# Five staging tiles instead of three for the first ten projection blocks of a transformer block

## The chip, the cores and the metric

The kernel runs on one core of a Trainium2 chip. The metric is the device time of one launch in microseconds (us): 2104.36, the median of three runs (2101.28 to 2106.47). The engines are called by their profile names where rows are read: PE is TensorE's matmul, PEld its weight load, DVE VectorE, ACT ScalarE, POOL GpSimd, SP SyncE. ACT and SP issue the DMAs of this kernel; SPq and ACTq in a row mean the issuing of a DMA by that engine.

## The reference

One pre-LayerNorm transformer block on a sequence of 2048 tokens of width 640: attention with 32 heads of width 20, then a SwiGLU feed-forward part of width 1728.

```python
def _A_ref(x, wqkv, wo):
    qkv = (x @ wqkv).reshape(B, S, 3, H, Dh).transpose(2, 0, 3, 1, 4)
    q, k, v = qkv[0], qkv[1], qkv[2]
    scores = jnp.einsum("bhqd,bhkd->bhqk", q, k) * (Dh ** -0.5)
    o = jnp.einsum("bhqk,bhkd->bhqd", _softmax(scores), v)
    return o.transpose(0, 2, 1, 3).reshape(B, S, D) @ wo
def _B_ref(x, w_gate, w_up, w_down):
    return (_silu(x @ w_gate) * (x @ w_up)) @ w_down
h = x + _A_ref(_layernorm(x), A_wqkv, A_wo)
return h + _B_ref(_layernorm(h), B_w_gate, B_w_up, B_w_down)
```

## The kernel before

Values in float32 are split into a high and a low part (`split`, L84: ACT copies the high part, another engine subtracts it for the low part), and a product is made of three matmuls: high by high, low by high, high by low.

The change lies in the first stage, the projections (L268 to L617). The 2048 tokens go through in four chunks (`c`, 0 to 3) of `CH` = 512. For each chunk the tokens are normalised on DVE (`norm`, L387), turned so that the width lies on the partitions (`flip`, L407; `flip_tokens`, L416, for the first chunk) and kept as two tiles `z_hi` and `z_lo` (`zs[c]`). From these come ten blocks of 128 rows of keys and queries (`query_key`, L434, 15 matmuls of 128x512; the first two blocks are made in `first_blocks`, L454), and eight half-tiles of values (`value`, L508, 15 matmuls of 128x320). A chunk has 18 slots, one for each piece of that work (`slot[0]`, L573); in chunk 0 slot 1 has no work, because blocks 0 and 1 are made in slot 0. Blocks have even numbers for keys and odd ones for queries.

*Staging tiles.* A finished block lies in a PSUM bank. `keep` (L469) takes the next staging tile from the list `es` (`next_e`, L264, pops the first and puts it at the end), copies the bank into it with ACT, splits it there into high and low, and queues its stores to the scratch tensors `q_d` and `k_d` in DRAM. Key blocks of chunks 0 and 1 also keep the difference of their two halves (`over`). Before slot 8 ACT and DVE split straight from PSUM; from slot 8 on ACT makes one copy first (L487) and POOL makes the low part. `flip` takes a staging tile too, as the place of its plain copy (L414, L281), and ACT and POOL read it right away; no DMA does. `es` has three tiles: `e0`, `e1` and a view on `v_stk0`, called `third`. In the fourth chunk `third` leaves the list and a tile of the pool's `z_hi` comes in (L570, L571).

```python
        def next_e():
            es.append(es.pop(0))
            return es[-1]
```

*Order of the stores.* `store` (L428) issues the pieces queued by the call before. So the stores of block m are issued when block m + 1 is kept. Up to slot 9 they go to SP's queue, later to ACT's (L505).

*Early maxima.* Scattered among these matmuls stand those of the score maxima. `visit` (L363) is called after each slot, and within a value or a block of later chunks; each call does up to two or three pairs. A pair is two matmuls into a double bank `ps_wide` (three of them). Pairs of the first head group use the full width, and DVE reduces 2x512 scores (`max_pair`, L171, L180); the others use the kept half sums and differences (`max_halves`, L182): ACT copies a half through relu (L193), DVE adds and reduces (L195). Their keys and queries are loaded back from `k_d` and `q_d` by SP into four `raw` tiles and the tile `fifth` (`load_items`, L302; `stack`, L141; L148). Four tiles of `raw` also hold the raw weights in the first slots (`load_w`, L373).

*What orders the work.* The program order on each engine is that of the calls; each engine takes its instructions strictly in that order, SP and ACT their DMA instructions as well. A tile is written again only after the reads of its former content, a store among them, have ended. [...]

After the projections come the attention with its output projection (PE and ACT), and the feed-forward part (PE), with PE nearly always busy.

Of the kernel before, what the change touches and what calls it, by code (L numbers as in the profile page):

```python
# [11 lines left out]
F32R = mybir.dt.float32r  # L12
# [5 lines left out]
P = 128  # L18
# [5 lines left out]
ND = D // P  # L24
NT = S // P
CH = 512
NC = S // CH
# [17 lines left out]
def tile_block(ctx: ExitStack, tc: tile.TileContext, x, wqkv, wo, wg, wu, wd, out):  # L45
# [30 lines left out]
    def ps_one():  # L76
        return psum.tile([P, CH], F32, name="ps_one", tag="ps_one", bufs=2)
# [6 lines left out]
    def split(src, hi, lo, lo_engine=nc.vector):  # L84
        nc.scalar.activation(hi, src, AF.Copy)  # L85
        lo_engine.tensor_tensor(out=lo, in0=src, in1=hi.bitcast(F32), op=ALU.subtract)  # L86

    def rstd_steps(pool, var, n, tag):

        v = pool.tile([P, n], F32, name="v_" + tag)  # L90
        r = pool.tile([P, n], F32, name="r_" + tag)
        t = pool.tile([P, n], F32, name="t_" + tag)

        def some(f, *args, **kw):
            return lambda: f(*args, **kw)

        ts, tt = nc.vector.tensor_scalar, nc.vector.tensor_tensor
        guess = [
            some(ts, v, var, EPS, None, op0=ALU.add),
            some(  # L100
                ts, r.bitcast(I32), v.bitcast(I32), -0.5, 1597463007.0, op0=ALU.mult, op1=ALU.add
            ),
        ]
        better = [
            some(tt, out=t, in0=r, in1=r, op=ALU.mult),
            some(tt, out=t, in0=t, in1=v, op=ALU.mult),
            some(ts, t, t, -0.5, 1.5, op0=ALU.mult, op1=ALU.add),
            some(tt, out=r, in0=r, in1=t, op=ALU.mult),
        ]
        return r, guess + better * 3  # L110
# [7 lines left out]
    def stats(pool, src, mv):  # L118
        st = pool.tile([P, 2, 6], F32, name="st")
        for i in range(2):  # L120
            nc.vector.bn_stats(st[:, i, :], src[:, i * HALF : (i + 1) * HALF])
        nc.vector.bn_aggr(mv, st)
# [29 lines left out]
    def load_keys(g, cs):  # L152

        k = keys[g] = k_stk[g % 2]
        stack(k[:, :, cs], 1, g, cs.start // CH)
# [103 lines left out]
    EW = CH + CH // 2  # L259
    es = [evp.tile([P, 2, EW], F32R, name=f"e{i}", bufs=1) for i in range(2)]  # L260
    es.append(v_stk[0].rearrange("p t w -> p (t w)")[:, : 2 * EW].bitcast(F32R))
    third = es[2] = es[2].rearrange("p (i n) -> p i n", i=2)

    def next_e():  # L264
        es.append(es.pop(0))
        return es[-1]

    with tc.tile_pool(name="pa", bufs=2) as pa:  # L268
        xs = {}
        zs = {}  # L270
# [3 lines left out]
        def load_x(c):  # L274
            for t in range(c * TPC, (c + 1) * TPC):
                xs[t] = pa.tile([P, D], F32, name="xt", tag="xt", bufs=4)
                nc.sync.dma_start(xs[t], x[t * P : (t + 1) * P, :])

        def split_sbuf(src, hi, lo, copy):

            nc.scalar.activation(copy, src, AF.Copy)  # L281
            split(copy, hi, lo, nc.gpsimd)
# [90 lines left out]
        def load_w(i):  # L373

            m, n = 2 * i, min(2, 3 * ND - 2 * i)
            raw = raw_tile().bitcast(F32)
            for j in range(n):
                raws[m + j] = raw[:, :, j * P : (j + 1) * P]
            nc.sync.dma_start(
                raw[:, :, : n * P], wqkv[:, m * P : (m + n) * P].rearrange("(k p) n -> p k n", p=P)  # L380
            )

        def split_w(m):
            cs = slice(m * P, (m + 1) * P)
            split(raws.pop(m), w_hi[:, :, cs], w_lo[:, :, cs])

        def norm(c):  # L387

            mv = pa.tile([P, TPC, 2], F32, name="mv")
            r, steps = rstd_steps(pa, mv[:, :, 1], TPC, "a")  # L390

            def apply(t):
                nc.vector.tensor_scalar(
                    xs[c * TPC + t], xs[c * TPC + t], mv[:, t, 0:1], r[:, t : t + 1],
                    op0=ALU.subtract, op1=ALU.mult,
                )

            zs[c] = (
                pa.tile([P, ND, CH], F32R, name="z_hi"), pa.tile([P, ND, CH], F32R, name="z_lo")
            )  # L400
            return (
                [lambda t=t: stats(pa, xs[c * TPC + t], mv[:, t, :]) for t in range(TPC)]
                + [lambda f=f, g=g: (f(), g()) for f, g in zip(steps[::2], steps[1::2])]
                + [lambda t=t: apply(t) for t in range(TPC)]
            )

        def flip(c, k):  # L407
            ps = ps_one()
            for t in range(TPC):
                nc.tensor.transpose(  # L410
                    ps[:, t * P : (t + 1) * P], xs[c * TPC + t][:, k * P : (k + 1) * P], ident
                )
            z_hi, z_lo = (z[:, k, :] for z in zs[c])
            split_sbuf(ps, z_hi, z_lo, next_e()[:, 0, :CH].bitcast(F32))  # L414
# [35 lines left out]
        def finish_keep():  # L450
            while halved:
                halved.pop(0)()

        def first_blocks(*hns):  # L454

            if not firsts:
                firsts.extend(ps_one() for _ in range(2))
            z_hi, z_lo = zs[0]
            for h, n in hns:
                cols = slice(h * CH // 2, (h + 1) * CH // 2)  # L460
                a, w = ((z_hi, w_hi), (z_lo, w_hi), (z_hi, w_lo))[n]
                for m, ps in enumerate(firsts):
                    for k in range(ND):
                        nc.tensor.matmul(
                            ps[:, cols], w[:, k, m * P : (m + 1) * P], a[:, k, cols],
                            start=(h == n == k == 0), stop=(h == 1 and n == 2 and k == ND - 1),
                        )
# [71 lines left out]
            nc.tensor.matmul(warm, ident, xs[TPC - 1][:, :CH], start=True, stop=True)  # L539
        for f in norm(0):  # L540
            f()
        first_raw = raws.pop(0), raws.pop(1)
        for m, raw in enumerate(first_raw):
            nc.scalar.activation(w_hi[:, :, m * P : (m + 1) * P], raw, AF.Copy)
# [19 lines left out]
        for c in range(NC):  # L564
            lns = []
            work = (some_keys + some_queries if c else first) + parts
            if c == NC - 1:
                work = some_keys + parts + some_queries

                es[:] = [e for e in es if e is not third]  # L570
                es.insert(1, pa.tile([P, ND, CH], F32R, name="z_hi")[:, :2])  # L571
            for j, (kind, *which) in enumerate(work):
                slot[0] = 18 * c + j  # L573
                if c == 0 and j < 9:
                    for i in range(split_at[j], split_at[j + 1]):
                        split_w(i + 2)
                        if i % 2 == 1 and loaded < 8:
                            load_w(loaded)
                            loaded += 1
                if j == 0 and c + 1 < NC:  # L580
                    if c > 0:
                        load_x(c + 1)
                    lns = norm(c + 1)
                if which:
                    if (c, j) == (0, 0):
                        first_blocks((0, 1), (1, 0), (1, 1), (0, 2), (1, 2))
                        for m, ps in enumerate(firsts):
                            keep(0, m, ps)
                    else:
                        (query_key if kind == "block" else value)(c, *which)  # L590
                visit(2 if kind == "value" or slot[0] < 10 else 3)
                finish_keep()
                if c == 0 and j == 6:
                    for ev in evs:
                        nc.gpsimd.memset(ev, 1.0)
                if j == (4 if c == 0 else 3):
                    load_keys(0, slice(c * CH, (c + 1) * CH))
                if j == (4 if c == 0 else 8) and c < 3:
                    load_queries(c)
                if 0 in ends:  # L600
                    finish_at = min(finish_at, slot[0] + 2)
                    if slot[0] == finish_at:
                        max_finish(0)
                if j == 14 and c == 3:
                    load_values(0)
                for _ in range(2 if j >= 5 else 1):
                    if j >= 1 and lns:
                        lns.pop(0)()
                if c + 1 < NC and 0 <= j - flip_at[c] < ND:
                    flip(c + 1, j - flip_at[c])  # L610
                if c == NC - 1 and j == 11:
                    nc.scalar.activation(
                        pa.tile([P, 1], F32, name="exp_table"), eps_t, AF.Exp
                    )
# [425 lines left out]
    for u in range(NU):  # L1040
        g, c = divmod(u, NC)
# [3 lines left out]
        for kt in range(NT):  # L1045
# [51 lines left out]
            k = 2 * (u - NU + 8)  # L1097
# [574 lines left out]
```

## Time and profile before

| | |
|---|---|
| runs | 2106.47, 2101.28, 2104.36 us; median 2104.36 |
| span of the profiled execution (first to last instruction) | 2102.6 us; its own time is not listed beside the span |
| mean granted PE clock | 0.996 of full speed |
| first chunk, slots 0 to 17 | ends near 97.8 us, where the first block of chunk 1 starts (PE L440 at 97.78) |
| projections | end near 388 us, where PE's attention rows (L964) begin |
| DMA | 305.38 MB in all, a mean of 145 GB/s |

A row of the timeline gives the start in us, the busy time, engine, line, operation, the tiles written and read, their shapes, the number of merged instructions, and in brackets how long the engine stood before and what released it. A row of the waits says which engine waited for which: total us, how often, and the longest.

### The profile page before, as it was taken

To read this page: it belongs to the slowest core of one execution; us is meant where nothing else is said; L and a number is where in the kernel's file an instruction comes from. 1 tells how busy PE (TensorE), PEld (TensorE's weight loads), DVE (VectorE), ACT (ScalarE), POOL (GpSimd) and SP (SyncE) were. 2 spreads that over 40 slices of the span, in tenths; PEclk is the share of its full clock that TensorE was granted. 3 is DMA by queue.
4 is the path that set the end of the run, shared out by engine and by line. 5 is a ranking of instruction groups with operands and counts; after the bars stand their busy time and mean duration, and the time that the engine had idled before them with its cause. 6 is when DMAs were issued, how large, how long until landed. Compare 5 with 4: busy or idle time off the path is not lost.

```text
span 2102.6 us, 37159 instructions
## 1 busy us (share of the span) xinstructions
PE 2063.2 (98%) x12636; PEld 1204.5 (57%) x12636; DVE 1659.2 (79%) x3631; ACT 1444.6 (69%) x2835; POOL 691.8 (33%) x949
## 2 busy tenths in 40 slices
PE   8899999999999999999999999999999999999998
PEld 6656566443333343333333333335578888888888
DVE  7677867788888888888888988887358666666677
ACT  4556575899999999999999999996743222212221
POOL 2131210234443434353420001001145444753555
PEclk9999999999999999999999999999999999999999
DMA  8575544335263443443631213132137755884542
GB/s 256 165 230 168 175 127 132 85 115 154 88 184 101 148 138 124 148 147 122 187 124 57 52 32 94 34 94 83 35 122 274 257 176 183 300 302 157 196 153 92
DMA packets 197285, 305.38 MB, mean 145 GB/s; under 512 B 47440, under 2 KB 82256, under 8 KB 196072
## 3 DMA queue, kind: packets, MB, share of 16 engines
q1 hardware_dynamic: 186168, 280.18, 42.0%
q10 hardware_dynamic: 10928, 22.82, 3.5%
q8 instruction: 102, 1.67, 0.3%
q14 instruction: 87, 0.71, 0.1%
HBM read 203.82 MB, written 98.30 MB: 144 GB/s over the span
## 4 chain that ended last, share of the span: by engine, by line
PE 88%; DVE 4%; DMA 3%; issue 1%; ACT 1%; POOL 1%; SPq 1%; ACTq 0%; POOLq 0%; DVEq 0%
PE acc L974 24%; PE ps_one L964 16%; PE ps_a L1135 15%; PE ps_max L204 12%; PE ps_b L1229 8%; PE ps_one L516 3%; PE ps_one L440 3%; PE ps_wide L188 3%; DVE over L195 2%; PE ps_max L695 2%; PE ps_b L695 1%; PE ps_wide L440 1%; DMA k_d<-e 1%; DMA halves<-j_d 1%; DVE mx L180 1%
## 5 line engine op out<-in xcount | busy, mean ns | idle before, releaser
L970 ACT ACTIVATE probs<-ps_one 128x512 f32<-128x512 f32 x2048 | 1056.7, 614 | 62.5 <-PE ps_one L964 37.1
L210 DVE TENSOR_REDUCE mx<-ps_max 128x1 f32<-128x512 f32 x1472 | 925.9, 684 | 108.2 <-PE ps_one L964 75.6
L964 PE MATMUL ps_one<-q_stk,k_stk 62*128 62x512 f32 x2048 | 586.1, 450 | 2.5 <-DVE m L86 1.8
L974 PE MATMUL acc<-probs,v_stk 128*32 128x512 f32 x4096 | 545.2, 604 | 0.0
L964 PEld LDWEIGHTS ps_one<-q_stk,k_stk 62*128 62x128 f32 x2048 | 251.3, 184 | 431.5 <-ACT probs L970 397.2
L204 PE MATMUL ps_max<-k_stk,q_stk 60*128 60x512 f32 x1472 | 380.8, 425 | 0.0
L204 PEld LDWEIGHTS ps_max<-k_stk,q_stk 60*128 60x128 f32 x1472 | 271.6, 186 | 25.3 <-DVE mx L210 1.2
L195 DVE CUSTOM_DVE_ANT_0 over<-ps_wide,over 128x256 f32<-128x256 f32 x512 | 185.4, 420 | 86.3 <-ACT over L193 85.9
L1350 DVE TENSOR_TENSOR tmp<-ps_a,tmp 128x512 f32<-128x512 f32 x208 | 141.1, 689 | 119.7 <-PE ps_a L1135 93.9
L193 ACT ACTIVATE over<-ps_wide 128x512 f32<-128x512 f32 x256 | 139.1, 597 | 90.5 <-PE ps_wide L188 44.1
L1229 PE MATMUL ps_b<-halves,yp 128*128 128x320 f32 x1032 | 179.3, 308 | 1.9 <-POOL yp L86 1.2
L974 PEld LDWEIGHTS acc<-probs,v_stk 128*32 128x32 f32 x4096 | 80.6, 108 | 175.4 <-issue 166.8
L1229 PEld LDWEIGHTS ps_b<-halves,yp 128*128 128x128 f32 x1032 | 165.1, 188 | 18.6 <-POOL yp L86 1.5
L1009 POOL TENSOR_TENSOR o<-o,rb 128x512 f32<-128x512 f32 x31 | 39.9, 1287 | 411.5 <-DMA q_stk<-q_d 163.6
L1135 PE MATMUL ps_a<-t,units 128*128 128x512 f32 x624 | 162.6, 396 | 0.0
L1135 PE MATMUL ps_a<-z,units 128*128 128x512 f32 x516 | 133.8, 394 | 0.0
L1135 PEld LDWEIGHTS ps_a<-t,units 128*128 128x128 f32 x624 | 112.6, 188 | 18.6
L86 POOL TENSOR_TENSOR yp<-y,yp 128x256 fp32r<-128x256 f32 x96 | 60.3, 628 | 188.0 <-ACT yp L85 188.0
L1234 DVE TENSOR_TENSOR h<-ps_b,h 128x320 f32<-128x320 f32 x248 | 110.0, 481 | 6.9 <-PE ps_b L1229 5.4
L1135 PEld LDWEIGHTS ps_a<-z,units 128*128 128x128 f32 x516 | 93.1, 187 | 15.9
L85 ACT ACTIVATE yp<-tmp 128x512 fp32r<-128x512 f32 x40 | 25.3, 632 | 103.2 <-POOL tmp L1222 103.2
L1135 PE MATMUL ps_a<-z,lasts 128*128 128x512 f32 x324 | 92.5, 393 | 0.0
(193 smaller groups left out, 2216.4 us busy)
## 6 DMA issues: line engine op xcount, KB each, us to landing
units<-w_d SPq DMA_DIRECT2D x186, 256.0 KB
w_d<-stage SPq DMA_DIRECT2D x106, 256.0 KB
halves<-j_d SPq DMA_DIRECT2D x70, 320.0 KB
j_d<-stage SPq DMA_DIRECT2D x42, 320.0 KB
k_stk<-k_d SPq DMA_DIRECT2D x64, 160.0 KB
q_stk<-q_d SPq DMA_DIRECT2D x64, 160.0 KB
rb<-r_d SPq DMA_DIRECT2D x32, 256.0 KB
raw<-k_d SPq DMA_DIRECT2D x42, 160.0 KB
```

The source lines that it names most:

```text
L193: nc.scalar.activation(over, ps[:, :, CH // 2 :], AF.Relu)
L195: nc.vector.tensor_tensor_reduce(over[:, b], ps[:, b, : CH // 2], over[:, b], 1.0, LOWEST, ALU.add, ALU.max, mx[:, b, pair, t, kc : kc + 1],)
L204: nc.tensor.matmul(ps, queries[u][rows, pair, t * P : (t + 1) * P], keys[u // NC][rows, pair, kc * CH : (kc + 1) * CH], start=True, stop=True,
L210: nc.vector.tensor_reduce(mxs[u][:, b, pair, t, kc : kc + 1], ps, axis=AX.X, op=ALU.max)
L440: nc.tensor.matmul(ps, w[:, k, m * P : (m + 1) * P], a[:, k, :], start=(n == 0 and k == 0), stop=(n == 2 and k == ND - 1),)
L964: nc.tensor.matmul(ps, keys[u // NC][rows, p, kt * P : (kt + 1) * P], queries[u][rows, p, :], start=True, stop=True,)
L970: nc.scalar.activation(probs[p][:, b, :], ps, AF.Exp, scale=scale)
L974: nc.tensor.matmul(acc[32 * j : 32 * j + 32, :], values[u // NC][:, kt, j * VW : j * VW + 32], probs[j // 2][:, j % 2, :], start=(kt == 0) ...
L1135: nc.tensor.matmul(ps.rearrange("p (t n) -> p t n", t=TPC), w[k][:, i], z[k][:, :, j], start=(first and m == 0), stop=(last and m == len(n ...
L1229: nc.tensor.matmul(ps, a, b, start=(n == 0), stop=(n == len(pairs) - 1))
L1234: nc.vector.tensor_tensor(out=h, in0=ps, in1=h, op=ALU.add)
L1350: add = lambda out, ps, x: nc.vector.tensor_tensor(out=out, in0=ps, in1=x, op=ALU.add)
```

## The change

The tiles for the flipped tokens get names of their own, one pair for even chunks and one for odd ones (`z_tiles`), in place of a pool of two of each. They are the same memory as before, and taken later: at the first flip of a chunk instead of when its normalisation is set up. At slot 0 of chunk 0 the pair of chunk 1 is put at the head of `es`, each cut to a staging tile's shape; at slot 10, when the ten blocks of chunk 0 have been kept, `es` is cut back to the three tiles that it had. Chunk 1's tokens are first flipped in slot 12.

```diff
+    own_es = es[:]
...
+        def z_tiles(c):
+            return tuple(
+                pa.tile([P, ND, CH], F32R, name=name, tag=f"{name}{c % 2}", bufs=1)
+                for name in ("z_hi", "z_lo")
+            )
...
-            zs[c] = (
-                pa.tile([P, ND, CH], F32R, name="z_hi"), pa.tile([P, ND, CH], F32R, name="z_lo")
-            )
...
         def flip(c, k):
+            if k == 0:
+                zs[c] = z_tiles(c)
             ps = ps_one()
...
             f()
+        zs[0] = z_tiles(0)
         first_raw = raws.pop(0), raws.pop(1)
...
                 es[:] = [e for e in es if e is not third]
-                es.insert(1, pa.tile([P, ND, CH], F32R, name="z_hi")[:, :2])
+                es.insert(1, z_tiles(NC)[0][:, :2])
...
+                if (c, j) == (0, 0):
+                    es[:0] = [
+                        t.rearrange("p k n -> p (k n)")[:, : 2 * EW].rearrange(
+                            "p (i n) -> p i n", i=2
+                        )
+                        for t in z_tiles(1)
+                    ]
+                if (c, j) == (0, 10):
+                    es[:] = [e for e in es if any(e is own for own in own_es)]
```

The tiles that the ten blocks of chunk 0 take, in the built order:

| block | 0 | 1 | 2 | 3 | 4 | 5 | 6 | 7 | 8 | 9 |
|---|---|---|---|---|---|---|---|---|---|---|
| before | e0 | e1 | third | e0 | e1 | third | e0 | e1 | third | e0 |
| changed | z_hi | z_lo | e0 | e1 | third | z_hi | z_lo | e0 | e1 | third |

The five flips of chunk 1 take e1, third, e0, e1, third before and e0, e1, third, e0, e1 after. The order of the instructions on every engine is the same in both. [...]

| DMA instruction on SP | waits for, before | waits for, changed |
|---|---|---|
| block 7's store, first piece | a load of raw (keys) | block 9's store on ACT, second piece |
| load into fifth (keys), fourth piece | block 7's store, first piece | the first store of values on ACT (`v_d`) |
| load of raw (queries), second piece | block 9's store on ACT, second piece | block 7's store, third piece |
| load of raw (keys), third piece | the first store of values on ACT (`v_d`) | block 8's store, second piece |

Block 8's store and the loads of raw stand behind the load into fifth on SP. From the loads of the second chunk's x (L277) on, the waits are the same ones again.

## The prediction

> **What bounds the kernel now.** The page first: TensorE is busy for nearly the whole span, so the only time a staging change can win is time in which TensorE stands still or runs at a lower clock.
>
> ```profile
> span 2102.6 us, 37159 instructions
> PE 2063.2 (98%) x12636; PEld 1204.5 (57%) x12636; DVE 1659.2 (79%) x3631; ACT 1444.6 (69%) x2835; POOL 691.8 (33%) x949
> ```
>
> Then the windows over the first chunk, which is where the change acts (columns: window, its length, busy time and instructions of PE, PEld, DVE, ACT and POOL, granted PE clock, DMA share, GB/s).
>
> ```profile
> 40.00:50.00 10.00, 9.44 (x41) 6.57 (x40) 5.58 (x10) 3.74 (x7) 2.64 (x4) 1.00 0.81 236
> ...
> 55.00:60.00 5.00, 2.85 (x18) 2.04 (x16) 0.89 (x1) 0.00 (x0) 0.00 (x0) 1.00 0.90 297
> 60.00:70.00 10.00, 5.55 (x18) 3.65 (x19) 7.36 (x18) 3.08 (x7) 1.27 (x1) 0.53 0.70 210
> ```
>
> From 55 to 70 us TensorE idles for 6.6 us (15 - 2.85 - 5.55), and its clock is 0.53 in the later ten. From 55 to 60 ScalarE does nothing, while the DMA is 90% busy. The table of waits between 40 and 110 us says for what.
>
> ```profile
> ACT e L487 <- DMA k_d<-e: 9.1, 1, 9.1
> ...
> PEld ps_wide L176 <- ACT e L85: 4.7, 1, 4.7
> ...
> ACT e L85 <- DMA k_d<-e: 4.0, 1, 4.0
> ```
>
> ScalarE waits twice for a store out of a staging tile: 4.0 us at block 7 and 9.1 us at block 9. With three tiles in rotation (e0, e1, third), block 9 takes the tile of block 6 and block 7 that of block 4. The chain of waits between 40 and 75 us shows why block 6's store is late.
>
> ```profile
> 46.51 4.58 DMA raw<-k_d
> ...
> 51.11 4.75 DMA raw<-k_d
> ...
> 55.88 4.21 DMA k_d<-e
> ...
> 60.24 0.60 ACT e L487
> ...
> 64.06 1.14 DVE mx L180
> ...
> 65.25 0.79 PE ps_wide L188 x2
> ```
>
> Block 6's store stands on SP's queue behind the loads of staged keys and queries. Its last piece leaves at 55.88 and lands 4.21 us later. Only then does ScalarE copy block 9 out. Everything behind that copy in ScalarE's order has waited with it, the relu copies (L193) above all; VectorE's maxima wait for those, and TensorE for the banks they hold. The timeline gives what that costs, slot by slot (start, busy time, engine, line, operation, idle time before and its releaser).
>
> ```profile
> 53.11 0.49 PE L176 MATMUL ps_wide<-k_stk,q_stk 60*128 60x512 f32 x2
> ...
> 54.14 0.47 PE L188 MATMUL ps_wide<-raw 60*128 60x512 f32 x1 [0.30 <-DMA raw<-k_d]
> ...
> 54.54 1.00 PE L516 MATMUL ps_one<-w_hi,z_hi 128*128 128x320 f32 x5
> ...
> 56.96 0.89 PE L516 MATMUL ps_one<-w_hi,z_lo 128*128 128x320 f32 x5
> ...
> 62.28 0.80 PE L176 MATMUL ps_wide<-k_stk,q_stk 60*128 60x512 f32 x2 [4.42 <-DVE mx L195]
> ...
> 65.97 1.70 PE L516 MATMUL ps_one<-w_hi,z_hi 128*128 128x320 f32 x5
> ...
> 72.04 1.01 PE L516 MATMUL ps_one<-w_hi,z_hi 128*128 128x320 f32 x5
> ...
> 76.55 0.98 PE L516 MATMUL ps_one<-w_hi,z_hi 128*128 128x320 f32 x5
> ...
> 80.57 0.66 PE L410 MATMUL ps_one<-ident,xt 128*128 128x128 f32 x4
> ...
> 80.98 0.97 PE L516 MATMUL ps_one<-w_hi,z_hi 128*128 128x320 f32 x5
> ```
>
> The five L516 rows with w_hi,z_hi are the starts of slots 10 to 14. Slot 13 takes 4.43 us (76.55 to 80.98) at full clock, and 0.41 of it (80.57 to 80.98) is the flip at its end. Slots 10 and 11 hold the same work without a flip: 15 value matmuls and two visits of two pairs, so 4.02 us undisturbed. Slot 10 takes 11.43 us (54.54 to 65.97), slot 11 6.07 (65.97 to 72.04). In slot 10 TensorE finishes the values at 57.85 (56.96 + 0.89) and stands for 4.42 us; afterwards it runs slowly: the same five matmuls take 1.70 us at 65.97 and 1.01 at 72.04, which is the clock.
>
> [...]
>
> **The change, part by part.** *Two more tiles for ten blocks.* With five in rotation (z_hi, z_lo of chunk 1, e0, e1, third), block 5 takes block 0's tile, block 7 block 2's, block 9 block 4's. Block 4's store has gone long before.
>
> ```profile
> 40.30 1.34 SPq L431 DMA_DIRECT2D k_d<-e  x2
> ```
>
> Its two pieces leave at 40.30 to 41.64, and even with the longest landing shown in that chain (4.75) they are done by 46.4; block 9's matmuls end at 53.11, where the next row starts, so the 9.1 us go. Block 2's store is older still, so the 4.0 us go. What this is worth on TensorE: slot 10 falls from 11.43 to 4.02 (-7.41) and slot 11 from 6.07 to 4.02 (-2.05), together **-9.46 us**.
>
> The 4.0 us at block 7 I price at nothing. TensorE is busy 9.44 of the 10 us there, so 0.56 bounds it above, and the start of slot 10 hangs on staged keys that have just landed (0.30 us of waiting on raw at 54.14), which no tile brings sooner. If that cover were gone it would be worth up to 0.56 more.
>
> *VectorE's queue.* The stall let VectorE drain. Without it, the maxima of slots 9 to 11, the normalisation of chunk 1 and the last weight splits come without a pause: it is busy 5.58 us in 40 to 50, 4.83 in 50 to 55, 0.89 in 55 to 60, 7.36 in 60 to 70, and all of this (18.7 us) now falls into some 20.5 (30 less the 9.46).
>
> ```profile
> 50.00:55.00 5.00, 4.70 (x21) 3.21 (x21) 4.83 (x12) 0.85 (x1) 2.32 (x2) 1.00 0.60 215
> ```
>
> At 91%, with three double banks between it and TensorE, a bank comes late now and then. Slots 10 and 11 hold three full-width maxima (the 1.14 us row of the chain) beside the cheaper half-width ones. Bounds: nothing, and two of these, 2.3 us. I take **+0.8**, under the middle, since VectorE also starts earlier by the 4.0 us that it no longer waits. Slot 12 then starts 8.66 us sooner.
>
> *What ScalarE's stores hold up on SP.* No instruction is added or removed and none changes its place, on any engine or queue; but in the built order some DMA instructions of SP wait for other ones than before. [...] Block 7's store (out of e0) waits for the second piece of block 9's store, and the last quarter of the load into fifth waits for the first store of values (v_d, issued in slot 12). Before, that second wait stood nine instructions later, on a load of raw. Behind the fifth load on SP stand block 8's store (out of e1) and the loads of the next queries. So e1 is freed only after a store of values has landed, and e1 is what the second flip (slot 13) copies into.
>
> ```profile
> 75.42 0.35 ACTq L431 DMA_DIRECT2D v_d<-ev  x1
> ...
> 81.30 0.61 ACT L281 ACTIVATE v_stk<-ps_one 128x512 f32<-128x512 f32 x1
> ```
>
> ```profile
> 80.97 0.66 SPq L148 DMA_DIRECT2D raw<-k_d  x2
> ```
>
> ```profile
> 84.12 0.60 PE L410 MATMUL ps_one<-ident,xt 128*128 128x128 f32 x4
> ```
>
> Before, the store of values left at 75.42 and the load that waited for it went at 80.97: 5.55 us. Shifted by 8.66 the store leaves at 66.8. By that row SP goes on at 72.3; block 8's two pieces follow with 0.33 us each (half of 0.66) and leave by 73.0; with 4.21 us to land, e1 is free at 77.2. ScalarE wants it at 72.6 (81.30 less 8.66) and would wait 4.6 us. What is late next is TensorE's third flip, which needs the bank that the copy empties: it comes at 75.5 (84.12 less 8.66) and would find it at 77.8 (77.2 plus 0.61), so 2.3 us lost. That is the upper bound by these rows. The lower is 0: another store of values left at 102.64 and its waiter at 105.03, 2.4 us, and with 2.4 twice e1 is free at 72.3, before it is wanted.
>
> ```profile
> 102.64 0.33 ACTq L431 DMA_DIRECT2D v_d<-ev  x1
> ...
> 105.03 1.79 SPq L277 DMA_DIRECT2D xt<-in_A_x  x4
> ```
>
> I take **+1.0**, the middle, since SP is held and moves less beside that store than it did at 75. Block 7's own store: ScalarE's piece leaves soon after the values of slot 10 (57.85), say at 58.5, and lands by 62.7 (4.21); three pieces follow within 2.99 us, as below, and land by 69.9. The first flip, a slot of 4.43 ahead of the second, wants e0 at 68.2, and has the same room of 2.2 us (75.5 less 72.6 and 0.61) ahead of the next bank: nothing.
>
> ```profile
> 56.22 2.99 SPq L431 DMA_DIRECT2D q_d<-e  x3
> ```
>
> [...]
>
> *Later chunks.* The order in which e0, e1 and third are taken shifts by one; each is taken at the same distance as before, so 0. The last chunk drops third from another place of the rotation, which has a tile reused one copy sooner after a flip, with no store in it: 0. The z tiles of chunk 1 are written from slot 12 on, after their stores (blocks 5 and 6) have left: 0.
>
> Sum: -9.46 + 0.8 + 1.0 = **-7.7 us**, so a span of 2094.9. The median of the three runs (2104.36) lies 1.76 above this span, which is taken as what lies around it: **2096.7**.
>
> **The rivals.** *The stall is half given back.* For it: VectorE's 91%, and e1 and the next queries at the far end of their landing times. Cost 2.3 + 2.3 by the upper bounds, and up to a third more if the loads behind block 8's store reach slot 15 late: the gain falls to between 3.3 and 4.9, the time to about 2100. Against it: ScalarE is idle enough to catch up.
>
> *A new stall of the old size* (the other side). The place is the second flip; its condition that the store of values and then block 8's store are each as slow as the slowest landing in the projections.
>
> ```profile
> 108.24 7.27 DMA k_d<-e
> ...
> 115.53 3.65 DMA raw<-q_d
> ```
>
> With 7.27 twice, e1 is free at 82.0 (66.8 + 7.27 + 0.7 + 7.27), TensorE idles 7.1 us (to 82.6 from 75.5) and pays for it afterwards again, 5.0 (9.46 less the 4.42 of first idle time). That is 12.1 lost against 8.66 won: 2107.8. It decides from an idle time of 3.7 us, a landing of e1 at 78.6, on. Against it: at 70 to 80 the DMA is at 31%, at 105 to 116 it was loading x. [...]
>
> ```profile
> 70.00:80.00 10.00, 10.00 (x58) 7.48 (x58) 6.60 (x34) 6.99 (x14) 1.29 (x1) 0.95 0.31 97
> ```
>
> *It doesn't do what it says*: ScalarE stops waiting, but TensorE is held at slots 9 to 12 by loads of raw that land no sooner (4.58 and 4.75 in the chain). Against it: the 0.30 at 54.14 is all that TensorE waited for them. Time about 2104.
>
> *More than the forecast*: chunk 1 has a stall of its own, from the 7.27 and 3.65 above, and in 119.3 to 126 the clock is low again; with other neighbours on the queue it could go: about 6 us, 2091. For it speaks only that timing moves.
>
> **How the numbers follow.** Forecast 0.62; half given back 0.21; new stall 0.08; no effect 0.05; more 0.04. What can't be told from no change is 0.3%, 6.3 us, so down to 2098.1: faster 0.64 (the forecast but for a tail of 0.05, some of the half given back, and the last case), slower than 2110.7 0.05 (the new stall with another in chunk 1), the rest 0.31. The forecast's own range is 2095 to 2099 (by its bounds, 2094.9 to 2099.5); the range reaches from the last case to the half given back and a little of the new stall: 2091.5 to 2103.
>
> **What would show it.** Right: no wait of ScalarE on a store between 40 and 60 us, granted clock 1.00 from 60 to 70, slot 12 at about 63.4 instead of 72.04. The coupling: block 7's store leaving after ScalarE's, and a wait of ScalarE on k_d<-e near 73. Wrong: a clock near 0.5 around 75 to 85, or a stall in chunk 1 that has grown by what was won.

## The result and the profile after

The changed kernel takes 2100.68 us (median of 20 runs, 2097.62 to 2103.08) where the kernel before takes 2104.19 us (20 runs, 2101.01 to 2106.86): a ratio of 0.998 with a 95% interval of 0.9974 to 0.9987. The gain is 3.5 us; the forecast was 7.7. The profiled execution has a span of 2099.6 us instead of 2102.6.

The head of the page of the changed kernel shows the same work as before:

```profile
span 2099.6 us, 37152 instructions
PE 2062.0 (98%) x12636; PEld 1204.8 (57%) x12636; DVE 1660.0 (79%) x3631; ACT 1444.2 (69%) x2835; POOL 691.7 (33%) x949
```

The windows of the changed kernel have the columns of those before (window, length, busy time and instructions of PE, PEld, DVE, ACT and POOL, granted clock, DMA share, GB/s):

```profile
40.00:50.00 10.00, 10.00 (x45) 7.16 (x44) 8.51 (x15) 4.24 (x8) 2.84 (x4) 1.00 0.80 250
...
55.00:60.00 5.00, 4.10 (x25) 2.88 (x23) 5.00 (x13) 1.63 (x3) 0.65 (x1) 1.00 0.86 245
60.00:70.00 10.00, 10.00 (x60) 7.10 (x56) 7.51 (x35) 7.05 (x13) 1.28 (x1) 1.00 0.55 169
70.00:80.00 10.00, 6.58 (x37) 5.08 (x37) 3.88 (x22) 5.16 (x10) 1.45 (x2) 0.86 0.70 198
80.00:90.00 10.00, 10.00 (x52) 7.28 (x51) 4.62 (x25) 6.12 (x12) 2.38 (x2) 0.79 0.40 145
```

Where the old stall was, from 55 to 70, TensorE now stands for 0.90 us only and keeps its full clock. The hole has come back fifteen microseconds later: 3.42 us of idle time from 70 to 80, and a clock at half from 77.3 to 84.1. The waits of the changed kernel between 40 and 130 us (engine waiting, for whom, total, times, longest) name it:

```profile
ACT e L283 <- DMA k_d<-e: 4.4, 1, 4.4
```

Neither the 9.1 us nor the 4.0 us of before is in that table. In their place ScalarE waits 4.4 us at L283, which is a flip, for a store of keys out of the staging tile that it wants to write. The chain of waits of the changed kernel (start, length, what) shows the path to it:

```profile
65.70 4.28 DMA v_d<-ev
70.00 0.27 SPq L148
...
70.38 0.31 SPq L438
...
70.73 5.20 DMA k_d<-e
...
76.03 0.61 ACT e L283
...
78.64 2.77 PE ps_one L523 x9
```

The first store of values leaves ScalarE's queue, lands 4.28 us later, and only then does SP issue the last piece of the load into `fifth` (L148). Block 8's store (L438) comes out right behind it at 70.38, its last piece lands at 75.93, and the second flip's copy follows. The timeline of the changed kernel (start, busy time, engine, line, operation, in brackets the idle time before and its releaser) and, below it, that of the kernel before for slots 15 and 16 and the start of chunk 1. The L523 rows with w_hi,z_hi are the starts of slots 10, 11, 12, 14, 15 and 16:

```profile
53.06 1.00 PE L523 MATMUL ps_one<-w_hi,z_hi 128*128 128x320 f32 x5
...
57.71 0.50 PE L188 MATMUL ps_wide<-raw 60*128 60x512 f32 x2 [0.90 <-DVE mx L180]
...
58.15 1.00 PE L523 MATMUL ps_one<-w_hi,z_hi 128*128 128x320 f32 x5
...
62.31 1.00 PE L523 MATMUL ps_one<-w_hi,z_hi 128*128 128x320 f32 x5
...
71.25 0.97 PE L523 MATMUL ps_one<-w_hi,z_hi 128*128 128x320 f32 x5
...
76.68 0.66 PE L417 MATMUL ps_one<-ident,xt 128*128 128x128 f32 x4 [2.12 <-ACT e L283]
...
78.64 1.70 PE L523 MATMUL ps_one<-w_hi,z_hi 128*128 128x320 f32 x5 [1.30 <-ACT ev L531]
...
85.36 0.98 PE L523 MATMUL ps_one<-w_hi,z_hi 128*128 128x320 f32 x5
...
93.84 1.42 PE L447 MATMUL ps_one<-z_hi,w_hi 128*128 128x512 f32 x5
```

```profile
84.81 1.00 PE L516 MATMUL ps_one<-w_hi,z_hi 128*128 128x320 f32 x5
...
89.30 0.97 PE L516 MATMUL ps_one<-w_hi,z_hi 128*128 128x320 f32 x5
...
97.78 1.43 PE L440 MATMUL ps_one<-z_hi,w_hi 128*128 128x512 f32 x5
```

Read as a ledger against the kernel before: slots 12 and 14 start 9.73 us sooner (62.31 for 72.04, 71.25 for 80.98), slot 15 6.17 (78.64 for 84.81), slot 16 3.94 (85.36 for 89.30), chunk 1 also 3.94 (93.84 for 97.78), and the end of the span 3.0. So 3.56 us went in slot 14, nearly all of it as idle time of TensorE (2.12 and 1.30), and 2.23 in slot 15, at half clock: the same five matmuls take 1.70 us instead of 1.00. The remaining 0.94 went after chunk 1's start.

### The profile page after: what moved, and what is told of

It reads as the page before. It is cut to its first block, busy times and chain, and to the rows that moved or that the text cites. A ratio compares the mean times of both kernels' runs of the same rounds, so it can differ in the third digit from the quotient of the medians.

```text
span 2099.6 us, 37152 instructions
## 1 busy us (share of the span) xinstructions
PE 2062.0 (98%) x12636; PEld 1204.8 (57%) x12636; DVE 1660.0 (79%) x3631; ACT 1444.2 (69%) x2835; POOL 691.7 (33%) x949
## 4 chain that ended last, share of the span: by engine, by line
PE 87%; DVE 5%; DMA 4%; issue 1%; ACT 1%; POOL 1%; SPq 0%; ACTq 0%; DVEq 0%; POOLq 0%
PE acc L991 24%; PE ps_one L981 15%; PE ps_a L1152 14%; PE ps_max L204 12%; PE ps_b L1246 7%; PE ps_one L523 3%; PE ps_one L447 3%; PE ps_wide L188 3%; DVE over L195 2%; PE ps_max L712 2%; PE ps_b L712 1%; DVE mx L180 1%; DMA t<-t_d 1%; PE ps_wide L447 1%; DMA k_d<-e 1%
```

## The experiments

Two theories stood against each other.

- A, *the held store*: block 8's store out of e1 is stuck on SP behind the fifth load, which waits for the first store of values; the second flip wants e1. What matters is which tile that flip takes.
- B, *the queue itself*: SP as a whole is late after the old stall is gone. To free e1 would only move the wait to the loads of raw behind block 8's store, or into chunk 1.

The expectations reckon with 9.9 us won by slot 12 and 6.2 lost again; by the ledger above it is 9.7 and 5.8.

The kernels of this section ran on two chips, each time with the kernel before on the same chip. It took 2103.45 us (24 runs) on the first, beside the first build of "the flips leave e1 alone", "block 8's store on ScalarE's queue" and the two with one more tile, and 2103.73 (24 runs) on the second, beside the other four. Starts given below are compared with those of the kernel before's trace.

**The flips leave e1 alone.** The flips take third and e0 in turn, the second of them e0, whose store has landed; e1 returns to the list at the next chunk.

```diff
                 if (c, j) == (0, 10):
-                    es[:] = [e for e in es if any(e is own for own in own_es)]
+                    es[:] = [own_es[2], own_es[0]]
+                if (c, j) == (1, 0):
+                    es[:0] = [own_es[1]]
```

> Two theories. A, the held store: the change wins some 9.9 us by slot 12 and loses 6.2 of it at the second flip of chunk 1, because block 8's store out of e1 stands on SP behind a load into fifth that waits for a store of values, and that flip copies into e1. B, the queue itself: SP is late as a whole, so the loads of raw that stand behind the same store are late too, and whatever frees e1 moves TensorE's wait to those loads in slot 15 or lengthens the stall of chunk 1. Here the five flips of chunk 1 take third and e0 in turn and leave e1 alone. A expects no wait of ScalarE on a store between 60 and 90 us, the granted clock at 1.00 from 70 to 90, slot 15 at about 75 instead of 78.64, and about 2095 us. B expects a wait of TensorE on raw near 76 to 80 us and about 2100.

Measured: 2097.37 us (7 runs), ratio 0.9973 (0.9962 to 0.9984). Its windows:

```profile
70.00:80.00 10.00, 9.91 (x62) 7.38 (x61) 5.87 (x32) 7.98 (x17) 2.99 (x3) 1.00 0.46 154
80.00:90.00 10.00, 9.70 (x57) 7.11 (x56) 6.07 (x33) 7.86 (x16) 2.56 (x2) 1.00 0.59 195
```

TensorE is busy 9.91 of 10 us from 70 to 80 and the clock stays at 1.00; slot 15 starts at 75.70 instead of 84.81, 9.1 us sooner, and chunk 1 8.4 (89.39). One thing is not as clean as it looks: in this build the load into `fifth` no longer waits for the store of values either (its four pieces take 2.27 us, 5.62 in the change), and block 8's store leaves at 65.67. The edit thus takes away both the hold on block 8's store and the need for e1. The hold itself has moved back, to a load of raw behind that store:

```profile
SPq L148 <- DMA v_d<-ev: 6.6, 1, 6.6
```

SP stands there from 71.6 to 78.2 us, and all that TensorE waits for raw afterwards, up to chunk 1, is 0.30 us (at 86.91). That speaks against B in this part of the kernel. The time is 2.4 us above the 2095 of A. The same kernel once more:

> The kernel whose flips leave e1 alone, beside the change on one chip: A, the held store, expects it 3 to 6 us faster than the change, near 2097, with no half clock between 60 and 100 us.

Measured: 2097.77 us (6 runs), ratio 0.9971 (0.9959 to 0.9983); slot 15 at 75.44, chunk 1 at 88.39. On this chip the change took 2100.2 us, so the gain over it is 2.4, just under the 3 to 6 of A. Both profiled executions are the fastest of their kernel's runs (2096.23 and 2093.59), so their spans are not set against medians. The medians gain about 6 us on the kernel before, some 2.5 more than the change.

**Block 8's store on ScalarE's queue.** The hold on SP stays; only the store is taken out from behind it.

```diff
-            sync = slot[0] < 10 or (c, m) == (NC - 1, 2 * ND - 1)
+            sync = slot[0] < 9 or (c, m) == (NC - 1, 2 * ND - 1)
```

> The changed kernel with block 8's store on ScalarE's queue instead of SP's; the flips take e0, e1, third as in the change, and the last quarter of the load into fifth still waits for the store of values, so SP and the raw loads behind it are held as before. A expects that e1 is free by 60 us, no wait at the second flip, and about 2095 us although SP is held until about 70. B expects about 2100, with TensorE waiting for raw or fifth in slot 15 near 76 to 80 us.

Measured: 2098.61 us (11 runs), ratio 0.9977 (0.9968 to 0.9986). Its timeline:

```profile
54.86 0.60 ACT L193 ACTIVATE over<-ps_wide 128x512 f32<-128x512 f32 x1 [1.55 <-issue]
...
59.40 0.69 PE L188 MATMUL ps_wide<-raw 60*128 60x512 f32 x2 [2.10 <-DVE mx L180]
...
60.02 1.70 PE L523 MATMUL ps_one<-w_hi,z_hi 128*128 128x320 f32 x5
...
65.22 1.01 PE L523 MATMUL ps_one<-w_hi,z_hi 128*128 128x320 f32 x5
...
66.84 6.70 SPq L148 DMA_DIRECT2D fifth<-k_d  x4
...
78.18 1.02 PE L523 MATMUL ps_one<-w_hi,z_hi 128*128 128x320 f32 x5
```

SP is held at `fifth` even longer than in the change (6.70 us for four pieces, 5.62 there), and yet slot 15 keeps what slot 12 had won: 6.8 us at slot 12 (65.22 for 72.04), 6.6 at slot 15 (78.18 for 84.81). So a held SP by itself cost TensorE 0.2 us between these two slots; it is the store behind it that costs. This is the cleaner evidence against B, since the flips still take e1. The time misses A's 2095, because a new wait stands ahead: ScalarE spends 1.55 us on issuing block 8's two pieces before its relu copy at 54.86, VectorE's maxima come after that copy, and TensorE stands for 2.10 us for one of them at 59.40 and runs at half clock for 3.4 us. So slot 12 wins 2.9 us less than in the change.

**The first flip takes e1.** This makes the need for e1 come one slot earlier.

```diff
-                    es[:] = [e for e in es if any(e is own for own in own_es)]
+                    es[:] = [own_es[1], own_es[0], own_es[2]]
```

> The changed kernel with e1 taken by the first flip instead of the second, so that the same late store is wanted one slot sooner: the dose is doubled. A expects ScalarE to wait 8 to 9 us on k_d<-e from about 67 to 76, TensorE to idle about 6 us from the second flip (70.8) on and then 7 to 10 us at half clock; of the 9.9 us won about 10 are lost: 2103 to 2106. B, in which e1 is not what binds, expects the change's time, 2100 to 2101.

Measured: 2102.82 us (11 runs), ratio 0.9991 (0.9983 to 1.0). Its timeline, and then its windows:

```profile
75.94 0.60 ACT L283 ACTIVATE e<-ps_one 128x512 f32<-128x512 f32 x1 [7.61 <-DMA k_d<-e]
...
78.65 0.80 PE L188 MATMUL ps_wide<-raw 60*128 60x512 f32 x2 [7.01 <-ACT ev L531]
```

```profile
70.00:80.00 10.00, 2.99 (x15) 2.02 (x14) 2.15 (x12) 3.49 (x7) 1.27 (x1) 0.74 0.62 185
80.00:90.00 10.00, 9.91 (x49) 7.69 (x47) 3.43 (x19) 5.73 (x12) 2.55 (x2) 0.75 0.36 102
```

e1 comes free at the same time as in the change (75.94 beside 76.03), but is wanted 3.4 us earlier, and nearly all of the gain is gone: slot 12 starts 8.7 us sooner (63.38), chunk 1 1.3 us later (99.05). This is the new stall of the prediction's rival, with its idle time (7.01; the rival had 7.1), made on purpose.

**The change itself beside these.** It ran again on the second chip, with no edit.

> The changed kernel as it is, on the same chip as the next three. Both theories expect 2100 to 2101 us, a wait of ScalarE on k_d<-e of 4 to 5 us near 72 to 76, and a half clock for some 7 us after it.

Measured: 2100.2 us (12 runs), ratio 0.9979 (0.997 to 0.9989). Its timeline:

```profile
74.44 0.60 ACT L283 ACTIVATE e<-ps_one 128x512 f32<-128x512 f32 x1 [2.75 <-DMA k_d<-e]
...
75.09 0.66 PE L417 MATMUL ps_one<-ident,xt 128*128 128x128 f32 x4 [0.53 <-ACT e L283]
...
77.05 1.70 PE L523 MATMUL ps_one<-w_hi,z_hi 128*128 128x320 f32 x5 [1.30 <-ACT ev L531]
```

The wait at the second flip is 2.75 us here where it was 4.35. The first store of values leaves at 65.7 us in both profiles, and the load into `fifth` ends at 68.65 here (62.30 and 6.35) and at 70.28 there (64.66 and 5.62): the size of the wait moves between executions, while the place stays. Both times the clock drops, at 77.1 us here and at 77.3 there, but for 3.4 us here and for 6.8 there. Both theories had expected 4 to 5 us and some 7.

**One more tile for block 9 alone.** The kernel before with one extra tile, taken for block 9 only and given back at slot 10. Block 7 still waits (3.0 us where it was 4.0), and the second flip takes third, in which block 8 now lies. The edit is against the changed kernel, so its own two tiles at slot 0 go out.

```diff
-                if (c, j) == (0, 0):
-                    es[:0] = [
...
-                    ]
+                if (c, j) == (0, 9):
+                    t = z_tiles(1)[1].rearrange("p k n -> p (k n)")[:, : 2 * EW]
+                    after = es[1:] + es[:1]
+                    es[:] = [t.rearrange("p (i n) -> p i n", i=2)] + es
                 if (c, j) == (0, 10):
-                    es[:] = [e for e in es if any(e is own for own in own_es)]
+                    es[:] = after
```

> The kernel before with one staging tile more for block 9 alone (z_lo of chunk 1), so the wait of 9.1 us goes and that of 4.0 us at block 7 stays. The prediction priced the latter at nothing to 0.56 us. Slot 12 at about 62.5 to 63.5 us (62.3 in the change, 72.0 before). Block 8 lies in third here, the second flip takes third, and in the built order the load ahead of its store waits for the same store of values: A expects the same stall there, 4 to 5 us of ScalarE, and about 2101 us, the change's time. If the 4.0 us had a share in the change's gain, slot 12 comes at 65 or later and the time is 2103 or more.

Measured: 2097.31 us (6 runs), ratio 0.997 (0.9958 to 0.9981). That is better than the change's two medians, which neither theory expected; the intervals of the ratios (0.997 to 0.9989 for the change in its second set of runs) overlap, so a real lead is likely and not shown. Its timeline:

```profile
75.47 0.60 ACT L283 ACTIVATE v_stk<-ps_one 128x512 f32<-128x512 f32 x1 [2.44 <-DMA k_d<-v_stk]
...
76.12 0.66 PE L417 MATMUL ps_one<-ident,xt 128*128 128x128 f32 x4 [0.22 <-ACT v_stk L283]
...
78.08 1.01 PE L523 MATMUL ps_one<-w_hi,z_hi 128*128 128x320 f32 x5 [1.31 <-ACT ev L531]
```

Slot 12 starts 8.4 us sooner (63.63), so block 9's wait alone is worth nearly all that the five tiles win there. TensorE comes 1.3 us later to the second flip than in the change, and the tile that this flip wants comes free 0.6 us sooner (75.47 for 76.03): TensorE stands for 0.22 and 1.31 us, and the clock holds (1.01 us for the five matmuls). Slot 15 then starts 6.7 us sooner. What was won less in the front was kept behind.

**One more tile for block 7 alone.** The same edit at slot 7, with the list restored at slot 8; here too the changed kernel's own two tiles go out.

```diff
-                if (c, j) == (0, 0):
-                    es[:0] = [
...
-                    ]
+                if (c, j) == (0, 7):
+                    t = z_tiles(1)[1].rearrange("p k n -> p (k n)")[:, : 2 * EW]
+                    after = es[1:] + es[:1]
+                    es[:] = [t.rearrange("p (i n) -> p i n", i=2)] + es
+                if (c, j) == (0, 8):
+                    es[:] = after
...
-                if (c, j) == (0, 10):
-                    es[:] = [e for e in es if any(e is own for own in own_es)]
```

> The kernel before with one staging tile more for block 7 alone, so the wait of 4.0 us goes and that of 9.1 us at block 9 stays. The prediction expects a gain of 0 to 0.56 us, about 2104, with slot 10 at 54 us and slot 12 at 71.5 to 72. The rival, that a drained VectorE queue and an earlier SP shorten the wait at block 9 too, expects a wait of ScalarE of 6 to 8 us there and 2100 to 2102.

Measured: 2104.25 us (11 runs), ratio 1.0007 (0.9998 to 1.0016). Its waits:

```profile
ACT e L494 <- DMA k_d<-e: 7.6, 1, 7.6
```

The 4.0 us at block 7 are gone, and block 9 still waits 7.6 us, 1.5 less than before, as the rival had it; the rival's 2100 to 2102 us did not come. In the trace slot 10 starts 0.9 us sooner (53.62), slot 12 and chunk 1 1.4 (70.64 and 96.37), and the span is 0.3 shorter. The median shows no gain. So this wait alone is worth nothing at the end, as priced, but up to chunk 1 it is worth more than the bound of 0.56.

**The first store of values on SP.** With this store on SP's queue, the fifth load can no longer wait for one on ScalarE's; the tiles are those of the change.

```diff
-                store()
+                store(queue=nc.sync if slot[0] == 12 else nc.scalar)
```

> The changed kernel with the first store of values on SP's queue instead of ScalarE's. In the built order it then stands behind block 8's store and the load into fifth waits for block 6's store alone; tiles and flips are those of the change. A expects block 8's store to leave at 65 to 66 us instead of 70.4, e1 free before the second flip wants it (71.7), no wait of ScalarE on it, slot 15 at about 75 and the time within 1 us of the kernel whose flips leave e1 alone, about 2097. If the landing of block 8's store, and not the hold on SP, is what makes e1 late, the wait stays above 3 us and the time is 2100.

Measured: 2094.42 us (5 runs), ratio 0.9948 (0.9936 to 0.996): 9.3 us under the kernel before and 5.8 under the change on the same chip. Its timeline, and then a window in chunk 1, below it the same window of the kernel before:

```profile
64.99 0.81 SPq L438 DMA_DIRECT2D k_d<-e  x2
...
71.75 0.36 SPq L438 DMA_DIRECT2D v_d<-ev  x1
...
72.30 0.60 ACT L283 ACTIVATE e<-ps_one 128x512 f32<-128x512 f32 x1
...
77.68 1.70 PE L523 MATMUL ps_one<-w_hi,z_hi 128*128 128x320 f32 x5 [1.94 <-ACT ev L531]
```

```profile
110.00:120.00 10.00, 9.81 (x45) 6.61 (x45) 7.25 (x37) 6.87 (x12) 5.08 (x4) 1.00 0.79 235
```

```profile
110.00:120.00 10.00, 6.92 (x31) 4.85 (x30) 5.08 (x24) 3.65 (x6) 4.38 (x3) 0.93 0.78 264
```

Block 8's store leaves at 64.99 instead of 70.38 and the second flip does not wait, as A says. But the store of values now stands behind the loads of raw on SP until 71.75, and ScalarE's next copy into that tile is late: TensorE stands for 1.94 us up to 77.68 and runs at half clock for 3.4 us. So slot 15 comes at 77.68 and not at the 75 of A, and by chunk 1 only 5.75 us are won (92.03). The rest of the gain lies later: in the profiled execution the stall of chunk 1 is gone, 9.81 us busy from 110 to 120 where the kernel before had 6.92. That was not the aim of the edit, and the time, below A's 2097, is lower for a reason that A does not have. It is the fastest version here, and it beats both kernels.

## Why the prediction was right and wrong

*The range held, the forecast did not.* The ratio's interval, a gain of 2.7 to 5.5 us, leaves out the forecast's 7.7. The time is that of the rival "half given back" (a gain of 3.3 to 4.9), and in part by luck: the rival put half of its loss on VectorE's queue, which cost 1.2 us, and had no drop of the clock. The prediction's own sign of being wrong, a clock near 0.5 around 75 to 85, came true.

*The old stall* was rightly placed, and its end won a little more than forecast: slot 12 starts 9.73 us sooner, where 8.66 was expected. Slots 10 and 11 take 5.09 us (53.06 to 58.15) and 4.16 (58.15 to 62.31); the two start rows are those of the same five matmuls in the changed kernel's trace. Undisturbed they were put at 4.02 each, so VectorE's queue cost 1.21 us, 0.90 of it in one wait for a maximum, where +0.8 was forecast between 0 and 2.3. Slot 10 began 1.48 us sooner (54.54 to 53.06), where nothing was forecast and 0.56 set as the bound. In the kernels here that run the same tiles up to block 9 that gain is 0.4 to 1.5 us, with block 9's tile alone it is 0.4 (54.18), with block 7's alone 0.9 (53.62). So up to one microsecond of it may belong to block 7; kernels with the same tiles scatter by as much, and it stays open.

*The term that failed is the "+1.0" for ScalarE's stores that hold up SP.* The mechanism was right at every joint: which load waits for which store, which store stands behind it, which flip wants the tile, and which of TensorE's instructions is late; the chain and the timeline after the change have them, from 65.70 to 78.64 us. The loss measured 5.8 us (3.56 in slot 14, 2.23 in slot 15): 2.12 and 1.30 us of idle time, and some 2.4 by the clock. Three things went into the difference.

1. The value taken. The upper bound, from the rows at 75 to 81, had the copy waiting 4.6 us and TensorE 2.3; measured were 4.35 and 2.12. The argument for the middle, that stores beside a held SP land sooner, is not borne out: the two landings, 4.28 and 5.20 us, add up to nearly what the upper bound took (5.55 and 4.21). The DMA share of 31% that the prediction held against slow landings was from a row of the kernel before; in the changed kernel the DMA is 70% busy from 70 to 80. In the second profile of the change the wait was 2.75 us, so the middle does occur, but it did not bring the cost down to 1.0.
2. What comes behind. The copies that ScalarE owed after L283, two relu copies and the values' (L531), came late as well, and TensorE stood a second time, 1.30 us. The bound stopped at the first instruction that was late.
3. The clock. The +1.0 and its upper bound priced idle time by its length alone; that was the author's estimate, and no run shows that a stall of some 2 us costs no more. Here the clock dropped at 77.3 us, 0.6 after the first idle piece of 2.12 us had ended, and stayed at half (0.50) for 6.8 us; the second piece lies within that time. In the kernel before, the clock dropped at 60.7 us, 2.8 us into the stall of 4.42 that began at 57.85. The prediction read only the mean of 0.53 from 60 to 70.

The window of the kernel before in which its clock drops, and then the windows of one microsecond of the changed kernel, show that third part:

```profile
60.00:61.00 1.00, 0.00 (x0) 0.00 (x0) 0.00 (x0) 0.76 (x2) 0.00 (x0) 0.84 0.85 252
```

```profile
76.00:77.00 1.00, 0.32 (x3) 0.32 (x4) 0.00 (x0) 0.94 (x2) 0.00 (x0) 1.00 0.60 197
77.00:78.00 1.00, 0.34 (x4) 0.10 (x1) 0.19 (x1) 1.00 (x3) 0.63 (x1) 0.64 0.57 195
78.00:79.00 1.00, 0.36 (x1) 0.36 (x2) 1.00 (x7) 1.00 (x3) 0.64 (x1) 0.50 0.88 279
...
84.00:85.00 1.00, 1.00 (x7) 0.40 (x6) 0.29 (x2) 0.61 (x2) 0.00 (x0) 0.95 0.63 209
```

*The cause is shown by removing it and by size.* Where the wait at the second flip is taken away without another put in its place (e1 left alone, block 8's store on ScalarE's queue), TensorE no longer stands behind that flip, and the clock holds there (1.00 from 70 to 80 us). With the wait at the flips at different lengths (one profile of each), the medians follow: no wait with e1 left alone, 2097.4 and 2097.8 us; 2.44 us, 2097.3; the change, 2.75 and 4.35 us in its two profiles, 2100.2 and 2100.7; 7.61 us, 2102.8. The two kernels that moved a store have no wait there either, and 2098.6 and 2094.4 us, with other stalls lost or won. By these medians the step lies where the clock begins to drop, between the waits of 2.44 and 2.75 us. The 20 runs of the change agree: the six with a mean granted clock of 0.998 or more took 2097.6 to 2099.2 us, the other fourteen, at 0.995 to 0.997, 2100.2 to 2103.1. This mean also holds chunk 1's stall, so which of the two stalls those six were spared is not shown.

*The rivals.* "Doesn't do what it says" fell with the first windows. "The new stall" did not come by itself; made on purpose, it cost 9.9 us of the first chunk (8.66 won at slot 13, 67.89 for 76.55, and 1.27 late at chunk 1), where the rival had 12.1. The end was 2102.8 us and not 2107.8; in the profiled execution chunk 1's own stall was absent (TensorE busy 9.96 of the 10 us from 110 to 120). "More" (2091, by chunk 1's stall going) is what the last experiment came near to.

*Later chunks at 0* is not settled. Of the 0.94 us lost after chunk 1's start, 0.80 go in its stall, in which TensorE waits for raw (the fourth block's row starts 3.91 us sooner, 109.69 for 113.60, the fifth's 3.11, 122.18 for 125.29). The row of the kernel before, and then that of the changed kernel:

```profile
119.31 1.62 PE L188 MATMUL ps_wide<-raw 60*128 60x512 f32 x5 [3.08 <-DMA raw<-q_d]
```

```profile
116.59 1.62 PE L188 MATMUL ps_wide<-raw 60*128 60x512 f32 x5 [4.22 <-DMA raw<-q_d]
```

In the other kernels this wait is between nothing and 4.4 us. So it moves by as much as the whole result between kernels that differ in chunk 0 only. It also bounds what can be said of B: freeing e1 moved next to nothing (0.30 us) to the loads of raw in chunk 0, but of the 5.8 us only about 2.5 reach the median, and what takes the rest was not isolated.

## What to carry to other kernels

When a stall is removed, follow the release chain to the next user of the same kind of tile and price it by the slowest landing nearby, then by what the late engine owes after it, and then by the clock. Where a load on one queue waits for a store on another, look in the built order at which store it is: what stands behind that load is the risk, and moving one small store was worth 5.8 us here beside the change, in part by chunk 1's stall, and choosing another tile for the next user 2.4, where the tiles themselves won 3.5. Try the part of a change that frees only the one wait on the path: one tile for one block gave no less here than two for ten.

## What was unexpected in the hardware

- The clock dropped after idle pieces of about 2 us and less. It was at half (0.50 in the windows of one microsecond) for 3.4 us after 2.10 us (block 8's store on ScalarE's queue), after 1.94 (the first store of values on SP), and after 0.53 and 1.30, with 0.66 us of matmuls between them (the change's second profile). It was at half for 6.8 us in the change's first profile, where the drop came after 2.12 us and another 1.30 fell into the half clock, and for 10.2 with the piece of 7.01, which began before the drop. Each length is twice what the granted clocks of the windows lack to 1.00, times their length; for the last, 2 x (0.26 + 0.25) x 10. After 0.22 and 1.31 us (block 9's tile alone) it did not drop (1.00 from 70 to 90).
- The lengths are 1, 2 and 3 times 3.4 us; why, no run here shows. Nor do the runs show how much idle time it takes. In the change's second profile 1.83 us in two pieces were followed by the drop, with block 9's tile alone 1.53 in two pieces by full clock, and with the first store of values on SP the drop came near 77.4 us, some 1.7 into the 1.94 (worked out from the granted clock of 0.87 from 70 to 80). These are single profiles.
- Two pieces of keys, 0.78 us of issuing, took 5.20 us to land with the DMA 70% busy from 70 to 80; the one piece of values before them took 4.28.
